# Attention and two MLPs in split fp32: query tiles and keys loaded a chunk ahead, differences in a tile of their own, weights converted in one stage

## The chip, the core and the metric

One Trainium2 chip, one of its cores. The metric is device time in microseconds (us) for one execution of the whole kernel. The core's engines run side by side, each with an instruction queue of its own that is worked off in order: TensorE (PE, matrix products), VectorE (DVE), ScalarE (ACT), GpSimd (POOL) and SyncE (SP), which in this kernel issues every DMA. An engine that stands at a semaphore holds up everything behind it in its own queue.

## What is computed

Attention of 8 heads over pooled keys and values, then two MLPs, all of it in fp32:

```python
k_p = k.reshape(B, H, S // 8, 8, D).mean(axis=3)         # B = H = 8, S = 576, D = 64
v_p = v.reshape(B, H, S // 8, 8, D).mean(axis=3)
attn = softmax(matmul(q, k_p.T) / sqrt(D))
x = matmul(attn, v_p).transpose(0, 2, 1, 3).reshape(4608, 512)
x = (sigmoid(x @ w_gate) * (x @ w_val)) @ w_out          # d_ff 1536
h = x @ w2_in                                            # d_ff 2048
out = (h * cos(h)) @ w2_out
```

The weights arrive as doubles.

## The kernel before

**Precision.** TensorE works on fp32r operands. Each fp32 number is held as a high and a low part, and a product is three matmuls: high x high, high x low, low x high. Making the two parts takes a copy on ScalarE (high) and a subtraction on VectorE (low). A weight block (128 x 512 doubles, 512 KB) takes more. ScalarE scales the exponents (`stage_exponent`, a Prelu, line 139), VectorE joins the bits (`stage_bits`, two operations, line 143), then come the high and the low part.

**Chunks and stages.** The 4608 tokens go in 9 chunks of 512. For each chunk, 12 gate steps (`gv_step`, line 515) compute 128 rows each of gate and value: 24 matmuls of 128x512 into two PSUM banks tagged "g" (four exist), a sigmoid on ScalarE, a product on VectorE. The attention of the next chunk is done beside these steps: `plan(c)` (line 580) gives for each of the 12 steps a list of calls, and the loop at line 1119 runs them behind the step's gate products. A chunk is made of the tail of one batch element and the head of the next, in 4 or 5 query tiles of up to 128 rows. For tile n at its step `at_[n]` there is `q_step` (load must be there; four transposes on TensorE, a copy qT on ScalarE), one step later `s_step` (scores; maxima and differences on VectorE, exponentials on ScalarE, the normalised a on VectorE), three steps after the first `a_step` (transposes of a; copies aT on ScalarE, low parts on VectorE). `x_step` then multiplies with the values (four products for a part of the chunk), and its results become xT. All of these use the four PSUM banks tagged "t", in turn. `q_load` is called three steps ahead of `q_step`, but not before step 0. Keys are loaded at step 0 in three groups (two of 64 pooled rows per head, one remainder of 8), pooled by GpSimd at step 1 (`kv_pool`), and transposed at step 2 (`k_step`). Values follow at steps 3 and 4.

**Differences.** For chunks 1 to 8, a gate block f and the block f + 6 are folded (`folded`, line 557). They are stored as quarters and as differences of quarters, for a product with seven instead of eight block products (`O_PRODUCTS`, line 700; the units are a third of such a product). GpSimd forms four differences, in place over the gate blocks, in two steps two ticks apart; three stores to `od` go out over three ticks. `afterwards(n, fn)` calls fn n ticks later, and a tick is a step.

**Weights converted early.** `far_weights` (line 176) is a generator. It loads a pair of blocks a and b of w2_out or w_out, converts them, forms sums of their quarters on GpSimd and converts these. One pair takes eight calls: 0 loads a; 1 loads b, Prelu of a; 2 Prelu of b; 3 bits; 4 sums, high part of a; 5 low part of a; 6 high part of b, high part of the first two sums; 7 low parts of b and of these, high part of the other two sums, whose low part opens the next call 0. The sums' results lie in the buffers of a and b, so the next pair's load waits for their store. `far_stores` issues the stores that are ready ahead of each call. Eight pairs of w2_out and six of w_out, 112 calls, run in chunks 1 to 7 at 16 a chunk (one in each step, two in each third one, lines 1143 to 1147).

**The last gate chunk and the new stage.** In chunk 8 there is no attention beside it. The blocks of w_out and w2_in are loaded there as doubles into buffers that come free, and converted beside the gate products (lines 1138 to 1151). Chunk 0's second product (`o_step`) runs there too, fed by `Ahead`, which fetches, splits and hands out blocks that were stored. Then the stage of h begins (line 1184): `h_step` for 16 blocks of each chunk, with the units of the folded product between them (`unit_go` fetches, splits and counts; `unit_step` multiplies; `due` says how many must be done by which block). The pool that held the blocks of `Ahead` is replaced by the pool of the units' operands (line 1169) when the gate stage has ended. At the end, `y_step` finishes chunk 0 of the output, and `y_chunk` does chunks 1 to 8 from seven products each. Their operands come through `strip_fetch`, `strip_high` and `strip_low`; `strip(n)` (line 917) converts up to job n and fetches one job more. `kept` (line 932) copies an accumulator out into a buffer of the ring "r", which the stored blocks y also use.

The loops that the change touches:

```python
 586      at_ = {5: (0, 2 if len(tail) == 1 else 1, 3, 5, 7), 4: (0, 2, 4, 6)}[len(tiles)]
 593          put(max(at_[n] - 3, 0), q_load, t)
1144                  for _ in range(1 + (at_f % 3 == 2)):
1145                      far_stores()
1146                      if next(far, far) is far:
1147                          load_all()
1228      strip(1)
```

Of the kernel before, what the change touches and what calls it, by code (L numbers as in the profile page):

```python
# [23 lines left out]
def attention_two_mlps(  # L24
# [22 lines left out]
    nc = tc.nc  # L47
# [39 lines left out]
    wd = [dp.tile([P, 2, DM], F32, name=f"wd{j}") for j in range(NF2)]  # L87
# [20 lines left out]
    order += [("o", f) for f in range(NF)] + [("i2", j) for j in PAIRED]  # L108
# [67 lines left out]
    def far_weights():  # L176

        def tile_(k, shape, dtype, name):
            return wp.tile(shape, dtype, tag=f"w{2 * NF + k}", name=name)

        def finished(k, kind, j, raw):
            t = tile_(k, [P, 2, DM], F32R, f"w{kind}_{j}")
            nc.scalar.copy(t[:, 0], words(raw, F32, 1))
            yield
            split_lo(nc.vector, t[:, 1], words(raw, F32, 1), t[:, 0])
            t = t.bitcast(F32)
            if kind == "o2":
                ready.append((wd[j], t))
            elif j < HF:
                ready.append((so[0][:, j], t[:, :, :HALF]))  # L190
            else:
                ready.append((so[5][:, j - HF], t[:, :, :HALF]))
                ready.append((so[6][:, j - HF], t[:, :, HALF:]))

        todo = [("o2", m, PAIRS) for m in range(PAIRS)] + [("o", m, HF) for m in range(HF)]
        for kind, m, step in todo:
            ja, jb = m, m + step
            a = load((wp, f"w{2 * NF}"), (kind, ja))
            yield
# [17 lines left out]
            for k, (op, x, y) in enumerate(sums):  # L217
                nc.gpsimd.tensor_tensor(out=t[:, k], in0=x, in1=y, op=op)
            yield from finished(3, kind, ja, a)
            yield  # L220
            both = finished(3, kind, jb, b)
            next(both)
            for k in range(2):
                c = tile_(k, [P, 2, 2, HALF], F32R, f"t{kind}{m}_{k}")
                nc.scalar.copy(c[:, :, 0], t[:, 2 * k:2 * k + 2])
                yield
                if k == 0:
                    next(both, None)
                split_lo(nc.vector, c[:, :, 1], t[:, 2 * k:2 * k + 2], c[:, :, 0])
                c = c.bitcast(F32)  # L230
                if kind == "o2":
                    ready.append((td[m][:, 2 * k:2 * k + 2], c))
                else:
                    ready.extend((so[1 + 2 * k + i][:, m], c[:, i]) for i in range(2))

    def split(upto=None, n=2):
# [13 lines left out]
        done["bits"] += len(some)  # L250

# [263 lines left out]
    def gv_step(c, f, half=None):  # L515
# [13 lines left out]
        s = gv.tile([P, C], F32, tag="s", name=f"s{c}_{f}_{cols.start}", bufs=2)[:, :n]  # L529
        nc.scalar.activation(s, pg[0], AF.Sigmoid)  # L530
# [3 lines left out]
        nc.vector.tensor_tensor(out=g[:, cols], in0=pg[1], in1=s, op=ALU.mult)  # L534
# [14 lines left out]
    def afterwards(n, fn):  # L549
        tasks.setdefault(clock[0] + n, []).append(fn)  # L550

    def tick():
        clock[0] += 1
        for fn in tasks.pop(clock[0], ()):
            fn()

    def folded(c, m, a, b):

        (a1, a2), (b1, b2) = ((x[:, :HALF], x[:, HALF:]) for x in (a, b))

        def less(out, x, y):
            nc.gpsimd.tensor_tensor(out=out, in0=x, in1=y, op=ALU.subtract)  # L562

        def put(n, t):
            nc.sync.dma_start(
                od[c][n:n + 2, :, m].rearrange("o p n -> p o n"), t.rearrange("p (o n) -> p o n", o=2)
            )

        def second():
            less(b2, b2, a1)  # L570
            less(b1, b1, b2)

        less(a1, a2, a1)
        less(a2, b2, a2)
        afterwards(1, lambda: put(5, b))
        afterwards(1, lambda: put(1, a))
        afterwards(2, second)
        afterwards(3, lambda: put(3, b))

    def plan(c):  # L580

        steps = [[] for _ in range(NF)]
        tiles = tiles_of(c)
# [36 lines left out]
        return steps  # L620
# [255 lines left out]
    def load_last():  # L876
# [4 lines left out]
        nc.sync.dma_start(t.bitcast(F32), wd[j])  # L881
# [153 lines left out]
    with tc.manual_schedule():  # L1035
# [82 lines left out]
        far = far_weights()  # L1118
        for c in range(NC):
            last = c == NC - 1  # L1120
            beside = [] if last else plan(c + 1)
            if last:
# [4 lines left out]
                load_all()  # L1127
# [3 lines left out]
            for at_f, f in enumerate(FOLDED if c else range(NF)):  # L1131
# [6 lines left out]
                elif last:  # L1138
                    if at_f >= 1:
                        go.go()  # L1140
                    split(len(raws) - 2)
                else:
                    split()
                    for _ in range(1 + (at_f % 3 == 2)):
                        far_stores()
                        if next(far, far) is far:
                            load_all()
                gv_step(c, f, 1 if c == 0 and f < FIRST else None)
                if last:
                    slots.extend(place[kind, f] for kind in "gv")  # L1150
                    load_all()
# [4 lines left out]
                if beside:  # L1156
                    for step in beside[at_f]:
                        step()
        while tasks:
            tick()  # L1160

# [3 lines left out]
        slots.extend((hp_, f"e{n}") for n in range(2))  # L1165
        load_all()
        o_homes.append((hp_, "e2"))
        last_slots.extend((hp_, f"e{n}") for n in (3, 0, 1))
        pp[0].release()
        pp[0] = tc.alloc_tile_pool(name="pp2", bufs=1, side="left", reuse_waits="tile")  # L1170
# [13 lines left out]
        for c in range(NC):  # L1184
# [8 lines left out]
            for k, j in enumerate(PAIRED):  # L1193
# [5 lines left out]
                if c == 0:  # L1199
                    split(n=1)  # L1200
                elif len(spare) < len(last_slots) and (c >= NC - 2 or k % 4 == 3):
                    load_last()
                late.append(h_step(c, j))
                if len(late) > 1:
                    late.pop(0)()
                if c < NC - 2:
# [15 lines left out]
        while tasks:  # L1222
            tick()
        load_combined(waiting.pop(0))
        while gy.next < len(gy.blocks):
            gy.go()
            y_step(*gy.take())
        strip(1)
# [37 lines left out]
```

## Time and profile before

| what | value |
|---|---|
| time, median of 3 runs (lowest to highest) | 1917.84 us (1917.09 to 1918.86) |
| the profiled execution | 1919.02 us, span 1917.2 us |
| TensorE matmuls, busy | 1789.3 us (93%), 8560 of them |
| TensorE weight loads, busy | 1491.5 us (78%) |
| VectorE, ScalarE, GpSimd, busy | 1155.9 us (60%), 928.3 us (48%), 533.2 us (28%) |
| mean granted clock of TensorE | 0.967 |
| moved by DMA | 391.20 MB, 204 GB/s |

The profile is of one execution. Busy time of TensorE is modelled and overlaps, so what counts there are the gaps and the clock. The granted clock is a share of full speed; it has two levels, 1.2 and 2.4 GHz, and a number between them is a mean over the stretch. Times of the trace are us from the start of the span. "Idle" is the time an engine stood before an instruction, with what released it behind an arrow. L66 is the line of the helper that forms all low parts.

### The profile page before, as it was taken

The page shows a single profiled execution, that of the slowest core. Times are in us where ns is not written, and L with a number is a line of the kernel's source. Part 1 is how long each engine was busy: PE and PEld are TensorE (multiplying, and loading weights), DVE is VectorE, ACT ScalarE, POOL GpSimd, SP SyncE. Part 2 cuts the span into 40 slices and gives each one's busy share as a digit, 9 for nine tenths or more (in the row PEclk, how much of TensorE's full clock was granted, in tenths as well). Part 3 has the DMA queues.
Part 4 walks back from the last instruction along what each step waited for, and adds up shares of the span by engine and source line. Part 5 has one row for each costly group of instructions (what it writes and reads, how often), then busy time and mean ns, then how long its engine had stood idle before and what let it go on. Part 6 is the DMA issues. An engine that isn't in the chain of part 4 may idle for free. (4 is left out here: it accounts for less than half of the span.)

```text
span 1917.2 us, 24961 instructions
## 1 busy us (share of the span) xinstructions
PE 1789.3 (93%) x8560; PEld 1491.5 (78%) x8560; DVE 1155.9 (60%) x1866; ACT 928.3 (48%) x1552; POOL 533.2 (28%) x656
## 2 busy tenths in 40 slices
PE   5879989898898989997999999999999998999999
PEld 4767868777777778875778888888887887888887
DVE  7675555455554645564666676676676655655665
ACT  6463434344343434343555555565564554444443
POOL 4104343535252522221001334334334441000000
PEclk8989989999999999998899999999999999999999
DMA  8424454545455544685677877777766688666664
GB/s 222 146 99 140 166 175 157 165 160 178 161 172 158 153 145 139 228 286 172 199 246 254 276 251 260 254 251 258 259 228 211 204 260 294 219 223 208 211 223 152
DMA packets 290782, 391.20 MB, mean 204 GB/s; under 512 B 55136, under 2 KB 231776, under 8 KB 290656
## 3 DMA queue, kind: packets, MB, share of 16 engines
q1 hardware_dynamic: 290656, 389.62, 62.8%
q8 instruction: 67, 1.10, 0.2%
q14 instruction: 59, 0.48, 0.1%
HBM read 242.22 MB, written 147.32 MB: 203 GB/s over the span
## 5 line engine op out<-in xcount | busy, mean ns | idle before, releaser
L534 DVE TENSOR_TENSOR g<-pv,s 128x512 f32<-128x512 f32 (+1 forms) x111 | 75.0, 676 | 282.5 <-PE pv L527 158.7
L820 DVE SCALAR_TENSOR_TENSOR r<-n,ph 128x512 f32<-128x512 int32 x144 | 98.9, 687 | 212.6 <-issue 97.8
L814 PE MATMUL ph<-x,wi 128*128 128x512 f32 x576 | 224.4, 390 | 0.0
L816 PE MATMUL ph<-x,wi 128*128 128x512 f32 x576 | 224.3, 389 | 0.0
L815 PE MATMUL ph<-x,wi 128*128 128x512 f32 x576 | 224.3, 389 | 0.0
L848 POOL TENSOR_TENSOR s<-r,r 128x256 f32<-128x256 f32 x64 | 76.1, 1189 | 467.0 <-DVE r L830 327.9
L826 ACT ACTIVATE r<-r 128x512 f32<-128x512 f32 x144 | 91.1, 633 | 236.2 <-DVE r L823 97.9
L525 PE MATMUL pg<-xT,wg 128*128 128x512 f32 (+1 forms) x444 | 188.2, 424 | 2.6 <-ACT e L443 2.6
L66 DVE TENSOR_TENSOR sp<-sf,sp 128x1024 fp32r<-128x1024 f32 x112 | 132.0, 1220 | 90.4 <-ACT sp L904 90.4
L526 PE MATMUL pg<-xT,wg 128*128 128x512 f32 (+1 forms) x444 | 179.6, 405 | 0.3 <-DVE xT L66 0.3
L527 PE MATMUL pg<-xT,wg 128*128 128x512 f32 (+1 forms) x444 | 178.6, 402 | 1.1 <-DVE wg L66 1.1
L527 PE MATMUL pv<-xT,wv 128*128 128x512 f32 (+1 forms) x444 | 170.6, 384 | 0.0
L525 PE MATMUL pv<-xT,wv 128*128 128x512 f32 (+1 forms) x444 | 170.4, 384 | 0.0
L526 PE MATMUL pv<-xT,wv 128*128 128x512 f32 (+1 forms) x444 | 170.4, 384 | 0.0
L904 ACT CAST sp<-sf 128x1024 fp32r<-128x1024 f32 x112 | 112.3, 1055 | 75.3 <-PE py_A L1007 28.6
L562 POOL TENSOR_TENSOR g<-g,g 128x256 f32<-128x256 f32 x96 | 75.7, 788 | 248.3 <-DVE g L534 139.9
L562 POOL TENSOR_TENSOR g<-g 128x256 f32<-128x256 f32 x96 | 73.4, 766 | 256.4 <-DMA od<-g 200.5
L814 PEld LDWEIGHTS ph<-x,wi 128*128 128x128 f32 x576 | 108.4, 188 | 22.6
L815 PEld LDWEIGHTS ph<-x,wi 128*128 128x128 f32 x576 | 108.3, 188 | 22.6
L816 PEld LDWEIGHTS ph<-x,wi 128*128 128x128 f32 x576 | 108.3, 188 | 22.5
L1002 PE MATMUL py_A<-tc,sp 128*128 128x512 f32 x384 | 120.6, 395 | 0.0
L530 ACT ACTIVATE s<-pg 128x512 f32<-128x512 f32 (+1 forms) x111 | 64.9, 584 | 100.3 <-PE pg L527 99.8
(180 smaller groups left out, 4227.6 us busy)
## 6 DMA issues: line engine op xcount, KB each, us to landing
sf<-sd SPq DMA_DIRECT2D x112, 512.0 KB
so<-so SPq DMA_DIRECT2D x84, 512.0 KB
uf<-od SPq DMA_DIRECT2D x168, 256.0 KB
od<-g SPq DMA_DIRECT2D x144, 256.0 KB
sd<-s SPq DMA_DIRECT2D x64, 512.0 KB
raw_o<-in_moe_w_out_dram SPq DMA_DIRECT2D x40, 512.0 KB
sd<-r SPq DMA_DIRECT2D x64, 256.0 KB
out_dram<-y SPq DMA_DIRECT2D x36, 256.0 KB
```

Of the source, the lines that this page charges most:

```text
L66: engine.tensor_tensor(out=lo, in0=x, in1=hi.bitcast(F32), op=ALU.subtract)
L525: nc.tensor.matmul(p, wh, x[:, 0, kb], start=kb == 0, stop=False)
L526: nc.tensor.matmul(p, wh, x[:, 1, kb], start=False, stop=False)
L527: nc.tensor.matmul(p, wl, x[:, 0, kb], start=False, stop=kb == KB - 1)
L562: nc.gpsimd.tensor_tensor(out=out, in0=x, in1=y, op=ALU.subtract)
L814: nc.tensor.matmul(p, wh, x[kb][:, 0], start=kb == 0, stop=False)
L815: nc.tensor.matmul(p, wh, x[kb][:, 1], start=False, stop=False)
L816: nc.tensor.matmul(p, wl, x[kb][:, 0], start=False, stop=kb == KB - 1)
L820: nc.vector.scalar_tensor_tensor(out=r, in0=n, scalar=-C1, in1=p, op0=ALU.mult, op1=ALU.add)
L826: nc.scalar.activation(r, r, AF.Sin, scale=0.5)
L904: nc.scalar.copy(t[:, 0, h * w:(h + 1) * w], got[c, n, h])
L1002: nc.tensor.matmul(p, x[:, 0, m, s], w, start=fresh and m == 0, stop=False, skip_group_check=True,)
```

## The change

- Query tiles 0 and 1 of a chunk are loaded at steps 9 and 10 of the chunk before, and key groups 0 and 1 at its step 10. Groups 0 and 1 are pooled at step 0, the remainder is still loaded at step 0 and pooled at step 1. (The plan of chunk 1 has all of these at step 0, as before.)
- GpSimd's four differences go into a tile t of their own, at the end of the next step; one store sends them two ticks later. The tile of the sigmoid is gone: it writes into g, and VectorE multiplies in place.
- `far_weights` also converts the eight pairs of w2_in (six calls a pair, no sums) and stores the finished w_out blocks whole. The calls come twice in each step of chunks 1 to 7, ahead of the gate products and behind them. `refill` then loads finished blocks in chunk 8, where nothing is converted any more.
- The pool of the units' operands is set up at the last step of chunk 8, and `unit_go` is called there twice and once behind it. `due` asks for the first units one h block later.
- `strip(1)` is called ahead of the last `y_step` instead of behind it.

```diff
+    wd = {
+        (kind, j): dp.tile([P, 2, DM], F32, name=f"w{kind}_{j}")
+        for kind, n in (("o2", NF2), ("o", NF), ("i2", NF2)) for j in range(n)
+    }
...
-    order += [("o", f) for f in range(NF)] + [("i2", j) for j in PAIRED]
...
-            if kind == "o2":
-                ready.append((wd[j], t))
-            elif j < HF:
+            ready.append((wd[kind, j], t))
+            if kind != "o":
+                return
+            if j < HF:
                 ready.append((so[0][:, j], t[:, :, :HALF]))
...
+        todo += [("i2", m, PAIRS) for m in range(PAIRS)]
...
             stage_bits([a, b])
             yield
+            if kind == "i2":
+                yield from finished(3, kind, ja, a)
+                both = finished(2, kind, jb, b)
+                next(both)
+                yield
+                next(both, None)
+                continue
...
+    refills = [("o", f) for f in range(NF)] + [("i2", j) for j in PAIRED]
+
+    def refill(tag):
+        kind, j = refills.pop(0)
+        t = wp.tile([P, 2, DM], F32R, tag=tag, name=f"w{kind}{j}")
+        nc.sync.dma_start(t.bitcast(F32), wd[kind, j])
+        blocks[kind, j] = t
+        place[kind, j] = wp, tag
...
-        s = gv.tile([P, C], F32, tag="s", name=f"s{c}_{f}_{cols.start}", bufs=2)[:, :n]
-        nc.scalar.activation(s, pg[0], AF.Sigmoid)
         g = halves.pop(f, None)
         if g is None:
             g = gv.tile([P, C], F32, tag="g", name=f"g{c}_{f}", bufs=4)
-        nc.vector.tensor_tensor(out=g[:, cols], in0=pg[1], in1=s, op=ALU.mult)
+        nc.scalar.activation(g[:, cols], pg[0], AF.Sigmoid)
+        nc.vector.tensor_tensor(out=g[:, cols], in0=pg[1], in1=g[:, cols], op=ALU.mult)
...
+    def tock():
+        for fn in tasks.pop((clock[0], True), ()):
+            fn()
...
-        less(a1, a2, a1)
-        less(a2, b2, a2)
-        afterwards(1, lambda: put(5, b))
-        afterwards(1, lambda: put(1, a))
-        afterwards(2, second)
-        afterwards(3, lambda: put(3, b))
+        def sums():
+            t = gv.tile([P, 4, HALF], F32, tag="t", name=f"tg{c}_{m}")
+            for k, x, y in ((0, a2, a1), (1, b2, a2), (3, b2, t[:, 0]), (2, b1, t[:, 3])):
+                nc.gpsimd.tensor_tensor(out=t[:, k], in0=x, in1=y, op=ALU.subtract)
+            afterwards(
+                2, lambda: nc.sync.dma_start(od[c][1:5, :, m].rearrange("o p n -> p o n"), t)
+            )
+        afterwards(1, lambda: nc.sync.dma_start(
+            od[c][5:7, :, m].rearrange("o p n -> p o n"), b.rearrange("p (o n) -> p o n", o=2)
+        ))
+        afterwards(1, sums, end=True)
...
+        def put_early(f, fn, *args):
+            early[f if c > 1 else 0].append(lambda: fn(*args))
+
         for n, t in enumerate(tiles):
-            put(max(at_[n] - 3, 0), q_load, t)
+            if n < 2:
+                put_early(NF - 3 + n, q_load, t)
+            else:
+                put(max(at_[n] - 3, 0), q_load, t)
         if c < B:
             for g in range(3):
-                put(0, kv_load, k, c, "k", g)
+                (put_early if g < 2 else put)(NF - 2 if g < 2 else 0, kv_load, k, c, "k", g)
                 put(3, kv_load, v, c, "v", g)
-                put(1, kv_pool, c, "k", g, nc.gpsimd)
+                put(1 if g == 2 or c == 1 else 0, kv_pool, c, "k", g, nc.gpsimd)
...
+        def far_step():
+            far_stores()
+            next(far, None)
+
+        plans = [plan(c) for c in range(1, NC)]
...
+            beside = [[] for _ in range(NF)]
+            if not last:
+                steps, early = plans[c]
+                for n in range(NF):
+                    if c == 0:
+                        beside[n] += early[n]
+                    beside[n] += steps[n]
+                    if c + 1 < NC - 1:
+                        beside[n] += plans[c + 1][1][n]
...
-                load_all()
+                for n in range(2 * NF, NSLOT):
+                    refill(f"w{n}")
...
                 elif last:
-                    if at_f >= 1:
-                        go.go()
-                    split(len(raws) - 2)
+                    if at_f == NF - 1:
+                        pp[0].release()
+                        pp[0] = tc.alloc_tile_pool(
+                            name="pp2", bufs=1, side="left", reuse_waits="tile"
+                        )
+                    (unit_go if at_f == NF - 1 else go.go)()
                 else:
                     split()
-                    for _ in range(1 + (at_f % 3 == 2)):
-                        far_stores()
-                        if next(far, far) is far:
-                            load_all()
+                    far_step()
                 gv_step(c, f, 1 if c == 0 and f < FIRST else None)
                 if last:
-                    slots.extend(place[kind, f] for kind in "gv")
-                    load_all()
+                    for kind in "gv":
+                        refill(place[kind, f][1])
...
+                    if at_f == NF - 1:
+                        unit_go()
+                elif c:
+                    far_step()
+                for step in beside[at_f]:
+                    step()
+                tock()
...
+            tock()
+        unit_go()
...
-                return min(TOTAL, -(-(k + 1) * TOTAL // (NF2 - 1)))
+                return max(0, min(TOTAL, -(-k * TOTAL // (NF2 - 2))))
...
-                if c == 0:
-                    split(n=1)
-                elif len(spare) < len(last_slots) and (c >= NC - 2 or k % 4 == 3):
+                if c and len(spare) < len(last_slots) and (c >= NC - 2 or k % 4 == 3):
...
             gy.go()
+            if gy.next == len(gy.blocks) - 1:
+                strip(1)
             y_step(*gy.take())
-        strip(1)
```

## Rows read from the trace of the kernel before

**Rows 1.** Waits of PE, whole span: line, released by, us in total, times, longest.
```profile
PE pq L386 <- DMA q<-in_q_dram: 31.9, 7, 5.7
PE pkr L332 <- POOL kR L286: 12.2, 6, 2.0
PE px L508 <- ACT qT L388: 8.6, 3, 6.8
```

**Rows 2.** Seven windows of the gate stage, PE: length, busy, granted clock, DMA share, GB/s.
```profile
168.00:183.00 15.00, 12.15 (x57) 0.89 0.49 129
236.00:272.00 36.00, 29.71 (x122) 0.86 0.73 214
330.00:366.00 36.00, 29.47 (x131) 0.91 0.76 223
423.00:462.00 39.00, 32.04 (x152) 0.96 0.71 214
515.00:556.00 41.00, 32.38 (x144) 0.88 0.67 198
606.00:650.00 44.00, 36.24 (x166) 0.88 0.65 188
708.00:728.00 20.00, 15.60 (x63) 0.83 0.69 216
```

**Rows 3.** Timeline of SP, steps 0 and 1 of chunk 2: start, length, issue.
```profile
237.56 0.39 SPq L174 DMA_DIRECT2D td<-to  x1
241.34 0.33 SPq L126 DMA_DIRECT2D raw_o<-in_moe_w_out_dram  x1
241.76 1.78 SPq L378 DMA_DIRECT2D q<-in_q_dram  x3
...
253.74 0.33 SPq L126 DMA_DIRECT2D raw_o<-in_moe_w_out_dram  x1
```

**Rows 4.** Timeline of PE and ACT, the same steps.
```profile
245.82 0.85 PE L386 MATMUL pq<-ident,q 128*128 128x128 f32 x4 [3.92 <-DMA q<-in_q_dram]
...
257.66 0.68 ACT L141 ACTIVATE raw_o<-raw_o 128x512 f32<-128x512 f32 x1 [0.75 <-DMA raw_o<-in_moe_w_out_dram]
```

**Rows 5.** Chunks 1 to 7, busy PE, PEld, DVE, ACT, POOL; two groups by form.
```profile
158.00:797.00 639.00, 589.30 (x2805) 487.06 (x2804) 346.99 (x686) 272.00 (x467) 257.84 (x330) 0.95 0.50 158
...
L141 ACT ACTIVATE raw_i<-raw_i 128x512 f32<-128x512 f32 x16 | 10.0, 665 | 0.0
...
L66 DVE TENSOR_TENSOR wi<-raw_i,wi 128x512 fp32r<-128x512 f32 x16 | 12.2, 785 | 0.0
```

**Rows 6.** Timeline of POOL, the key remainder of chunk 3, in step 1.
```profile
261.09 1.76 POOL L286 TENSOR_TENSOR raw_k<-raw_k 64x256 f32<-64x256 f32 x2
262.93 0.65 POOL L286 TENSOR_TENSOR kR<-raw_k 64x64 f32<-64x64 f32 x1
```

**Rows 7.** Waits of SP's queue and of ACT, whole span: total, times, longest.
```profile
SPq L126 <- DMA td<-to: 60.5, 16, 5.3
...
ACT raw_o L141 <- DMA raw_o<-in_moe_w_out_dram: 37.0, 18, 5.8
```

**Rows 8.** The stage of h begins: timeline of PE and SP, and a window of PE.
```profile
909.53 0.80 PE L770 MATMUL po_A<-up,so 128*128 128x512 f32 x1 [13.69 <-ACT up L730]
...
902.12 2.12 SPq L739 DMA_DIRECT2D uf<-od  x4
...
905.00:942.00 37.00, 28.72 (x100) 0.77 0.62 205
```

**Rows 9.** The stage of y begins: timeline of PE and ACT; DMA, 1570 to 1620.
```profile
1604.35 1.22 PE L1002 MATMUL py_B<-tc,sp 128*128 128x512 f32 x2 [5.95 <-ACT sp L904]
...
1611.93 0.63 PE L1002 MATMUL py_A<-tc,sp 128*128 128x512 f32 x2
...
1607.83 1.17 ACT L935 COPY m<-py_A 128x512 f32<-128x512 f32 x2 [2.59 <-DMA out_dram<-y]
...
DMA packets 7346, 16.03 MB, mean 321 GB/s; under 512 B 590, under 2 KB 4046, under 8 KB 7343
```

More of the change, by code (lines that the diff above doesn't have):

```diff
@@ L86, in attention_two_mlps @@
     sd = {c: dp.tile([7, P, PAIRS, HALF], F32, name=f"sd{c}") for c in range(1, NC)}
-    wd = [dp.tile([P, 2, DM], F32, name=f"wd{j}") for j in range(NF2)]
+    wd = {
+        (kind, j): dp.tile([P, 2, DM], F32, name=f"w{kind}_{j}")
+        for kind, n in (("o2", NF2), ("o", NF), ("i2", NF2)) for j in range(n)
+    }
     td = [dp.tile([P, 4, 2, HALF], F32, name=f"td{m}") for m in range(PAIRS)]
@@ L547, in attention_two_mlps, with afterwards @@
     clock = [0]
-    def afterwards(n, fn):
-        tasks.setdefault(clock[0] + n, []).append(fn)
+    def afterwards(n, fn, end=False):
+        tasks.setdefault((clock[0] + n, end), []).append(fn)
     def tick():
         clock[0] += 1
-        for fn in tasks.pop(clock[0], ()):
+        for fn in tasks.pop((clock[0], False), ()):
+            fn()
+    def tock():
+        for fn in tasks.pop((clock[0], True), ()):
             fn()
@@ L559, in folded @@
         (a1, a2), (b1, b2) = ((x[:, :HALF], x[:, HALF:]) for x in (a, b))
[L561 to L566, printed above, removed]
-            )
-        def second():
-            less(b2, b2, a1)
-            less(b1, b1, b2)
-        less(a1, a2, a1)
-        less(a2, b2, a2)
-        afterwards(1, lambda: put(5, b))
-        afterwards(1, lambda: put(1, a))
-        afterwards(2, second)
-        afterwards(3, lambda: put(3, b))
+        def sums():
[4 more added lines that the diff above has]
+                2, lambda: nc.sync.dma_start(od[c][1:5, :, m].rearrange("o p n -> p o n"), t)
+            )
+        afterwards(1, lambda: nc.sync.dma_start(
+            od[c][5:7, :, m].rearrange("o p n -> p o n"), b.rearrange("p (o n) -> p o n", o=2)
+        ))
+        afterwards(1, sums, end=True)
     def plan(c):
         steps = [[] for _ in range(NF)]
+        early = [[] for _ in range(NF)]
         tiles = tiles_of(c)
@@ L619, in plan @@
             put(f, fn, *args)
-        return steps
+        return steps, early
     x2 = {}
@@ L1118, in attention_two_mlps @@
         far = far_weights()
+        def far_step():
+            far_stores()
+            next(far, None)
+        plans = [plan(c) for c in range(1, NC)]
         for c in range(NC):
             last = c == NC - 1
-            beside = [] if last else plan(c + 1)
-            if last:
+            beside = [[] for _ in range(NF)]
[7 more added lines that the diff above has]
+                        beside[n] += plans[c + 1][1][n]
+            else:
                 far_stores()
@@ L1155, in attention_two_mlps @@
                         o_next()
-                if beside:
-                    for step in beside[at_f]:
-                        step()
+                    if at_f == NF - 1:
[5 more added lines that the diff above has]
+                tock()
         while tasks:
             tick()
+            tock()
+        unit_go()
         gv.release()
         hp_ = tc.alloc_tile_pool(name="hp", bufs=1, side="right", reuse_waits="tile")
-        slots.extend((hp_, f"e{n}") for n in range(2))
-        load_all()
         o_homes.append((hp_, "e2"))
         last_slots.extend((hp_, f"e{n}") for n in (3, 0, 1))
-        pp[0].release()
-        pp[0] = tc.alloc_tile_pool(name="pp2", bufs=1, side="left", reuse_waits="tile")
         TOTAL = len(O_PRODUCTS) * STEPS
@@ L1223, in attention_two_mlps @@
             tick()
+            tock()
         load_combined(waiting.pop(0))
```

3 lines of the change are left out of this document (2 added, 1 removed).

## The prediction

> **What bounds the kernel now.** I read first the waits of TensorE, then the windows around the stalls, then the queues that feed them. TensorE is the bound: everything that is computed goes through it, and no product is added or taken away. So the change is worth what it takes off TensorE's idle time and off the stretches that follow at the lower clock. [rows 1] shows two waits that come back once a chunk: the transposes of a query tile wait for its load (31.9 us in 7 times; the first, in the opening, is not touched here), and the transpose of the key remainder waits for GpSimd's pooling (six times, up to 2.0 us). [rows 2] has the seven stretches of the gate stage around these waits. In each row the length less PE's busy time is idle time, and the length times what the granted clock lacks to 1.0 is what the lower of the two levels (1.2 instead of 2.4 GHz) costs. Idle: 2.85 + 6.29 + 6.53 + 6.96 + 8.62 + 7.76 + 4.40 = 43.4 us. Clock: 1.65 + 5.04 + 3.24 + 1.56 + 4.92 + 5.28 + 3.40 = 25.1 us. Together **68.5 us**. [rows 3] and [rows 4] show why the query is late: the load leaves SyncE's queue at 241.76, inside the step that needs it, behind a weight load that itself waited for a store.
>
> **The sum is made against the profiled execution**, 1919.0 us with a span of 1917.2; it stands 1.2 us above the median of the three runs, 1917.84.
>
> **Part 1: query tiles 0 and 1 and key groups 0 and 1 loaded a chunk ahead.** q moves from step 0 to steps 9 and 10 of the chunk before, two or three steps early, where a step takes 639 / 84 = 7.6 us [rows 5]. The four transfers and more pass the stores of the same queue, but a late q now has some 15 us of slack. The query wait ends. Keys 0 and 1 land two steps early and are pooled in step 0, so GpSimd has only the remainder left in step 1: 1.76 + 0.65 = 2.4 us [rows 6]. The remainder's load stays in step 0, though, and in chunks 2 to 5 both weight calls of that step now stand ahead of it on SyncE. Before, the first blocked SyncE until 241.34 and the second came a step later (until 253.74, [rows 3]). After, the second store wait, 3.8 us in the mean and 5.3 at most [rows 7], comes at once: the load leaves near 248, lands about 4 us later and is pooled near 254.5. TensorE reached that transpose 2.0 us before 263.58, at 261.5, and will reach it some 6 us earlier without the query stall: 255.5. Margin 1 us. Taken: **-68.5, and +3** for remainders that are late; bounds 0 and 4 x (2.0 + 1.6) = 14.
>
> **Part 2: differences in their own tile.** The same four GpSimd operations, one store of four quarters instead of two of two; GpSimd no longer waits for a store before it overwrites, and SyncE's store waits for nothing late (two ticks behind). The sigmoid now writes into g's buffer, so ScalarE waits for a buffer of four; its last reader, the differences, ran two steps earlier. Nothing on the path: 0, covered by GpSimd's idle time, 639 - 258 us [rows 5].
>
> **Part 3: all weights converted in the gate stage.** Sixteen w2_in blocks move there: two ScalarE operations of 0.67 us and three VectorE operations of at most 0.79 each [rows 5], 21 us and at most 38 us, in a stretch where these engines idle 367 and 292 us. As work they are hidden. The twelve w_out blocks are no longer converted twice. What matters is the **spacing of the calls**. A pair of w_out or w2_out blocks takes eight calls; these came 16 to a chunk and now come two in every step, one ahead of the gate products and one behind. Call 0 loads block a, after a wait for the store of the tile that held its buffer; call 1 loads b and puts a's Prelu on ScalarE. Before, a whole step lay between a load and its Prelu; now half of one does. Store 3.4 us (237.56 + 0.39 to 241.34), load 3.9 us (253.74 to 257.66) [rows 3, 4]: the chain of 7.3 us starts only when the last step's g is done, and the Prelu reaches ScalarE 3.8 us later. So ScalarE stands some 3.5 us in call 1, and about as long in call 2 for block b (store and load again, against half a step). The longest such wait so far is 5.8 us, all of them 37.0 [rows 7]. Behind ScalarE's wait queue the sigmoid (four banks, two steps of cover), the copy qT, the exponentials and the copies aT.
>
> TensorE meets it where a step has five users of the four "t" banks: one query tile and four x products, the fifth of which needs qT's copy done. That is so in chunk 1 (step 4) and chunk 2 (step 5), and in chunks 3 and 4 the x products wait for aT a step behind. The kind of wait exists already: px behind qT, 8.6 us in three times [rows 1]. Taken: 4 chunks x (2.6 us idle + 1.4 us clock) = **+16**. Bounds: 0, as the slack may hold; 45, if each of the 13 pairs after the first passes the 3.5 us on. From chunk 5, step 8, the calls are for w2_in, whose loads wait for no store: 0.
>
> The Trainium skill, page "SBUF — State Buffer", section "The DMA setup-cost knee", gives a transfer about 2 us plus its bytes at 436 GB/s; my estimate from it is 3.2 us for 512 KB, 6.4 us for the chain. By that page the lag would be 1 us smaller and this term +12. The measured 3.4 and 3.9 us decide.
>
> **Part 4: the new product's operands sooner.** TensorE stands from 895.8 to 909.5, 13.7 us [rows 8]: the first fetch leaves SyncE at 902.12, behind stores and raw loads. Now it leaves a step earlier, ahead of chunk 8's last gate products, and the first units come after two blocks of h, not one. In the window 905 to 942 there are 8.3 us idle, 4.5 of them the same wait, so 3.8 more; clock 0.23 x 37 = 8.5 us, of which 2.3 fall in the idle part. Total 13.7 + 3.8 + 6.2 = 23.7. The second unit's fetch still leaves behind the last weight load, which waits for TensorE, and is 1 to 4 us late. Taken **-21**; bounds -24 and -10.
>
> **Part 5: strip(1) ahead of the last y_step.** The wait of product B, 5.95 us, ends. But the next product (py_A at 1611.93) needs accumulator A copied out, and that copy started only at 1607.83, behind the store of y whose buffer it takes [rows 9]. Its own operand is converted behind that copy on ScalarE. The move puts strip(1)'s fetch, 1 MB, ahead of those stores on SyncE, in a stretch where the DMA engines moved 321 GB/s [rows 9]: about 3 us later. So the copy starts near 1610.7, the product near 1614, not at 1611.93; the wait goes from B to A and grows. Taken **+2**; bounds -8 (B's wait and its clock gone, nothing behind it) and +6 (twice the fetch).
>
> **Sum:** -68.5 + 3 + 16 - 21 + 2 = -68.5; 1919.0 - 68.5 = 1850.5, and 1.2 lower on the scale of the median: **1849 us**.
>
> **Rivals.**
> Clean: ScalarE's waits stay covered, term 3 is 0, the remainder is never late, the stage start gives 23.7. -68.5 - 23.7 + 2 = -90: **1828**. For it: in 37.0 us of such waits so far TensorE stood for little. Against: half the distance. Chance 0.25.
> Not what it says: hoisted loads still leave late, as SyncE is in order and stands in every fourth step for two stores. Then the query wait stays, 26.9 us and some 13 of the clock: 1849 + 40 = **1889**. Against: two steps of slack. Chance 0.06.
> Slower: ScalarE's waits for converted weights become TensorE's in every pair. It decides when a pair costs TensorE over 84.5 / 14 = 6.0 us (84.5 being the gain without the 16 of part 3). At both longest waits [rows 7], 5.8 + 5.3, less 3 of slack, it is 8.1 x 14 = 113, and 1918 - 84.5 + 113 = **1946**. For it: PSUM has two steps of cover and no more. Against: ScalarE is idle 57% of the stage. Chance 0.05.
>
> **How the numbers follow.** The forecast has 0.60, clean 0.25, the two others 0.11, 0.04 lies elsewhere. All bounds at their best give 1919 - 68.5 - 24 - 8 - 1 = 1817, at their worst -68.5 + 14 + 45 - 10 + 6 = -13.5, 1904. The range 1815 to 1888 holds the forecast, the clean case and the lower half of the bad end. A measurement of this kernel tells apart about 0.2%, 4 us. Faster: forecast, clean, not-what-it-says and most of the rest, 0.93; same 0.02; slower 0.05.
>
> **What would show it.** Right: no wait of pq for q beyond the first 5 us, key remainder waits near nothing; px waits of 2 to 4 us behind qT or aT in chunks 1 to 4; longer waits of ScalarE's Prelu for raw_o; po_A's first wait under 4 us; no wait of py_B, but one of 8 to 11 us ahead of py_A's second product. Wrong: the pq waits still there; gate stretches without any px wait (then 1828); a wait at each fourth step; py_A's second product at once.

## The result and the profile after

The changed kernel takes **1942.72 us** (median of 4 runs, 1939.25 to 1949.19) against 1918.21 for the kernel before (4 runs, 1917.09 to 1918.86): a ratio of **1.0132, interval 1.0105 to 1.0159**. It is slower, by 24.5 us or 1.3%, and the interval lies wholly above 1. 1849 was forecast.

| profiled execution | before | after |
|---|---|---|
| time; span | 1919.02; 1917.2 us | 1939.25; 1937.4 us |
| VectorE, ScalarE, GpSimd, busy | 1155.9, 928.3, 533.2 us | 1128.1, 908.8, 548.7 us |
| mean granted clock | 0.967 | 0.962 |
| moved by DMA | 391.20 MB, 204 GB/s | 414.28 MB, 214 GB/s |

The work of VectorE and ScalarE became less, as the change says, and the time did not. The stages tell where. These are the windows of TensorE after, cut at the first gate product of a chunk, the first product of h and the first of y (start:end, length, busy, granted clock, DMA share, GB/s): chunks 1 to 5, chunks 6 and 7, chunk 8, the stage of h, the stage of y.

```profile
151.60:654.30 502.70, 431.92 (x2022) 0.92 0.60 191
654.30:821.30 167.00, 164.34 (x792) 0.98 0.57 181
821.30:919.18 97.88, 97.88 (x433) 1.00 0.76 249
919.18:1609.07 689.89, 672.77 (x2930) 0.99 0.75 246
1609.07:1937.40 328.33, 315.54 (x1793) 0.98 0.64 211
```

Cut in the same way, the kernel before has these; the first line counts 421.04 us busy at a clock of 0.96:

```profile
152.20:608.60 456.40, 421.04 (x2024) 0.96 0.52 162
608.60:793.00 184.40, 170.06 (x793) 0.94 0.48 151
793.00:892.96 99.96, 98.29 (x434) 1.00 0.77 255
892.96:1592.68 699.72, 674.22 (x2930) 0.98 0.74 245
1592.68:1917.20 324.52, 314.39 (x1793) 0.99 0.64 213
```

Four differences are gains or small: -17.4 in chunks 6 and 7, -2.1 in chunk 8, -9.8 in the stage of h, +3.8 at the end. One decides: **chunks 1 to 5 grew by 46.3 us**. There TensorE stands 35.4 us longer (502.70 - 431.92 against 456.40 - 421.04), and the same products (2022 and 2024 records of them) count 10.9 us more of busy time, at a granted clock of 0.92 instead of 0.96.

The waits of TensorE after (line, released by, us in total, times, longest) show which wait went and which came:

```profile
PE pg L545 <- ACT xT L529: 30.8, 5, 7.8
PE psc L419 <- ACT qT L408: 16.9, 4, 7.3
...
PE px L528 <- ACT qT L408: 12.8, 3, 6.8
...
PE pq L406 <- DMA q<-in_q_dram: 3.4, 1, 3.4
```

The query's wait of [rows 1], 31.9 us, is down to the 3.4 us of the opening, and the key remainder's 12.2 us are gone. In their place stand the first gate product of a chunk, which waits for ScalarE's copy xT, and the scores, which wait for ScalarE's copy qT: 47.7 us together. The waits of ScalarE say why these copies are late:

```profile
ACT raw_o L143 <- DMA raw_o<-in_moe_w_out_dram: 108.1, 24, 9.3
...
ACT raw_i L143 <- DMA raw_i<-in_moe_w_in_dram: 42.2, 13, 6.0
...
ACT wo L185 <- DMA so<-wo: 29.8, 6, 8.1
ACT wo L185 <- DMA wo<-wo: 29.4, 6, 8.5
```

The Prelu (L143) waits 108.1 us for doubles of w2_out and w_out that are not there yet (37.0 in [rows 7]) and 42.2 for those of w2_in. The high-part copies (L185) wait for stores that must leave their target first, 29.8 and 29.4 us. Before, these two were:

```profile
ACT wo L183 <- DMA wd<-wo: 29.2, 8, 6.3
...
ACT wo L183 <- DMA so<-wo: 13.7, 4, 6.0
```

The first of the five stalls, at the end of chunk 1, can be followed instruction by instruction. ScalarE, VectorE, SyncE and TensorE (start, length, line, operation; in brackets how long it stood before it and for what):

```profile
233.22 0.65 ACT L143 ACTIVATE raw_o<-raw_o 128x512 f32<-128x512 f32 x1 [7.75 <-DMA raw_o<-in_moe_w_out_dram]
...
246.04 0.66 ACT L185 CAST wo<-raw_o 128x512 fp32r<-128x512 f32 x1 [8.50 <-DMA wo<-wo]
...
249.19 0.62 ACT L236 CAST to<-to 128x512 fp32r<-128x512 f32 x1 [1.49 <-DVE wo L66]
249.72 1.61 ACT L529 CAST xT<-px 128x384 fp32r<-128x384 f32 x4
...
238.64 1.22 DVE L66 TENSOR_TENSOR wo<-raw_o,wo 128x512 fp32r<-128x512 f32 x1
...
236.20 4.05 SPq L319 DMA_DIRECT2D raw_k<-in_k_dram  x4
...
241.00 0.36 SPq L176 DMA_DIRECT2D wo<-wo  x1
...
250.24 0.79 PE L545 MATMUL pg<-xT,wg 128*128 128x512 f32 x1 [7.27 <-ACT xT L529]
```

Read from below. TensorE stands 7.27 us for xT. xT is an eviction (a copy out of PSUM) of 1.6 us, but it stands in ScalarE's queue behind the weight calls 6 and 7. The copy of call 6 waited 8.50 us for the store of block a, which had to leave the buffer that block b's copy writes. That store left SyncE at 241.00, behind the issues of the hoisted key loads (4.05 us). The low part that it carries was ready at 239.86, so the place in SyncE's queue cost it 1.1 us at most. From the end of its issue it took 4.7 us. Of the 7.27 us, 3.1 pass while ScalarE still stands at that copy, and 3.7 with what comes between it and xT: the two copies of sums, a sigmoid and a further wait of 1.49 us.

### The profile page after: what moved, and what is told of

The parts are those of the page before. It is cut to its first block, busy times and chain, and to the rows that moved or that the text cites. A ratio compares the mean times of both kernels' runs of the same rounds, so it can differ in the third digit from the quotient of the medians.

```text
span 1937.4 us, 24756 instructions
## 1 busy us (share of the span) xinstructions
PE 1794.7 (93%) x8560; PEld 1496.4 (77%) x8560; DVE 1128.1 (58%) x1830; ACT 908.8 (47%) x1528; POOL 548.7 (28%) x656
## 2 busy tenths in 40 slices
DMA packets 296350, 414.28 MB, mean 214 GB/s; under 512 B 55072, under 2 KB 231712, under 8 KB 296224
## 5 line engine op out<-in xcount | busy, mean ns | idle before, releaser
L553 DVE TENSOR_TENSOR g<-pv,g 128x512 f32<-128x512 f32 (+1 forms) x111 | 75.1, 676 | 336.8 <-ACT g L552 141.4
L545 PE MATMUL pg<-xT,wg 128*128 128x512 f32 (+1 forms) x444 | 188.4, 424 | 35.2 <-ACT xT L529 30.8
L872 POOL TENSOR_TENSOR s<-r,r 128x256 f32<-128x256 f32 x64 | 76.1, 1188 | 453.6 <-DVE r L854 328.3
L545 PEld LDWEIGHTS pg<-xT,wg 128*128 128x128 f32 x444 | 89.3, 201 | 54.2 <-ACT xT L529 31.9
L840 PEld LDWEIGHTS ph<-x,wi 128*128 128x128 f32 x576 | 108.1, 188 | 22.5
L839 PEld LDWEIGHTS ph<-x,wi 128*128 128x128 f32 x576 | 108.1, 188 | 22.4
L552 ACT ACTIVATE g<-pg 128x512 f32<-128x512 f32 (+1 forms) x111 | 64.9, 585 | 116.6 <-PE pg L547 61.2
L847 DVE SCALAR_TENSOR_TENSOR r<-n,r 128x512 f32<-128x512 int32 x144 | 107.8, 749 | 5.0
```

Source lines behind the costliest of these rows:

```text
L545: nc.tensor.matmul(p, wh, x[:, 0, kb], start=kb == 0, stop=False)
L839: nc.tensor.matmul(p, wh, x[kb][:, 1], start=False, stop=False)
L840: nc.tensor.matmul(p, wl, x[kb][:, 0], start=False, stop=kb == KB - 1)
L847: nc.vector.scalar_tensor_tensor(out=r, in0=n, scalar=-C2, in1=r, op0=ALU.mult, op1=ALU.add)
```

## The experiments

Each ratio is to executions of the kernel before on the same chip; experiment 6 was executed once and has none. The stages are cut as above, each from one profiled execution.

**1. The change without part 3.** The calls come 16 a chunk again, and w_out and w2_in are converted beside the last gate chunk and the first h blocks again. The first theory: the new pace of the weight calls and their new places cost the time. The rival: the hoisted loads do, by standing ahead of the weight stores on SyncE and in the DMA engines.

```diff
-        todo += [("i2", m, PAIRS) for m in range(PAIRS)]
...
-                    far_step()
+                    for _ in range(1 + (at_f % 3 == 2)):
+                        far_stores()
+                        if next(far, far) is far:
+                            load_all()
...
-                elif c:
-                    far_step()
```

> The kernel after with part 3 undone: w_out and w2_in are converted beside the last gate chunk and the first h blocks again, and the calls of the weight generator come 16 a chunk, ahead of the gate products. Theory 1 (the pace of the calls: ScalarE stands for stores and loads of weight blocks, and TensorE behind it): the stretch of chunks 1 to 5, 503 us after and 456 us before, falls to about 400 to 415, and the time to 1835 to 1855 us. Theory 2 (the loads that were moved ahead stand on SyncE and in the DMA engines in front of the weights' stores): the waits of ScalarE for stores stay long, and the time stays above 1900 us.

Measured 1859.03 us, ratio 0.9702 (0.9676 to 0.9727). That is above the 1835 to 1855 expected; the window of chunks 1 to 5 is as expected. That window, and waits of TensorE and ScalarE:

```profile
151.70:566.00 414.30, 407.39 (x2023) 0.99 0.56 179
...
PE pg L544 <- ACT xT L528: 4.7, 3, 1.9
...
ACT raw_o L144 <- DMA raw_o<-in_moe_w_out_dram: 30.7, 20, 5.4
```

So part 3 costs 84.6 us of span (1937.4 - 1852.8): 88.4 in chunks 1 to 5, and 3.8 come back elsewhere. The 88.4 are 63.9 more idle time (70.8 against 6.9) and 24.5 more busy time at the lower clock. The rest of the change is worth some -60 us: -58 by the medians, -64.4 by the two profiled spans.

**2. The change without the hoist**, the rival's own test.

```diff
-            if n < 2:
-                put_early(NF - 3 + n, q_load, t)
-            else:
-                put(max(at_[n] - 3, 0), q_load, t)
+            put(max(at_[n] - 3, 0), q_load, t)
...
-                (put_early if g < 2 else put)(NF - 2 if g < 2 else 0, kv_load, k, c, "k", g)
+                put(0, kv_load, k, c, "k", g)
```

> The kernel after with part 1 undone: all q and k loads in their own chunk again, pooling at step 1. Theory 1: the waits for weight blocks stay, the waits for q and for the key remainder come back on top: 1955 to 1985 us. Theory 2: the wait of the xT copies at the chunk's end (31 us in five times) goes, the q waits (27 us) come back: 1930 to 1945 us.

Measured 1965.76 us, ratio 1.0257 (1.0234 to 1.028): 23 us slower than the change, not faster. TensorE waits for the query again, and for xT still. Below these two waits stand the store of block a and the copy behind it at the end of chunk 1:

```profile
PE pq L406 <- DMA q<-in_q_dram: 32.3, 5, 8.6
PE pg L545 <- ACT xT L529: 20.6, 5, 4.9
...
242.34 0.33 SPq L176 DMA_DIRECT2D wo<-wo  x1
...
245.05 0.65 ACT L185 CAST wo<-raw_o 128x512 fp32r<-128x512 f32 x1 [5.07 <-DMA wo<-wo]
```

The rival falls as the main cause. It has a share: without the hoist the xT waits come to 20.6 us instead of 30.8, and this store takes 2.4 us from the end of its issue instead of 4.7. At the ends of chunks 2 to 4 the copy gets its buffer 2.4 to 2.7 us from the end of the last store's issue here, and 4.7 to 5.3 us after. So the hoisted loads lengthen the transfer of these stores; their place in SyncE's queue cost the first 1.1 us at most.

**3. The pace alone**: experiment 1 with its 112 calls once ahead of the gate products and once behind, and no w2_in and no whole w_out blocks.

```diff
-                    for _ in range(1 + (at_f % 3 == 2)):
-                        far_stores()
-                        if next(far, far) is far:
-                            load_all()
+                    far_stores()
+                    next(far, None)
...
+                elif c:
+                    far_stores()
+                    next(far, None)
```

> e1_weights_as_before, but its 112 weight calls (w2_out and w_out only, no w2_in, no whole w_out blocks) come twice in each step, one ahead of the gate products and one ahead of the attention, as in the kernel after; they are through in chunk 5. If the pace is the cause: chunks 1 to 5, 414 us in e1 and 503 after, come out at 480 to 505, and the time at 1925 to 1950 us. If what was added (sixteen blocks of w2_in, the whole stores of w_out) is the cause: chunks 1 to 5 under 430, 1855 to 1880 us.

Measured 1926.55 us, ratio 1.0036 (1.0022 to 1.005), chunks 1 to 5 at 488.70, as the theory of the pace expected:

```profile
151.40:640.10 488.70, 432.84 (x2023) 0.92 0.57 178
...
PE pg L544 <- ACT xT L528: 24.8, 4, 7.2
...
ACT raw_o L144 <- DMA raw_o<-in_moe_w_out_dram: 101.5, 25, 7.8
```

Of the 88.4 us, 74.4 (488.7 - 414.3) come with the pace alone; the other 14 come with the blocks of w2_in and the whole w_out stores. The work that was added is the smaller part of the cost. The pace is two things that this run doesn't part: the calls stand half a step apart, and all 112 of them fall into chunks 1 to 5, where experiment 1 has 80.

**4. Both calls of a step behind the attention work**, at the change's pace. The work stays; what differs is what stands behind the calls on ScalarE, and the distance between the two calls of a step.

```diff
-                    far_step()
...
-                elif c:
-                    far_step()
...
+                if c and not last:
+                    far_step()
+                    far_step()
```

> The kernel after with both weight calls of a step put behind the step's attention work (they were one ahead of the gate products, one ahead of the attention). Nothing else. Theory 1: the copies qT, aT and xT no longer stand behind a Prelu or a copy that waits for a DMA in the same step; the waits of TensorE for xT (30.8 us) and qT (29.7 us) shrink to under a third, 1880 to 1910 us. Theory 2: stores and loads are as late as before, and so is ScalarE: within 10 us of 1943.

Measured 1881.11 us, ratio 0.9807 (0.9787 to 0.9828), 62 us faster than the change. Chunks 1 to 5, ScalarE's waits for weight blocks, and TensorE's for qT:

```profile
152.90:600.00 447.10, 420.68 (x2023) 0.96 0.65 209
...
ACT raw_o L143 <- DMA raw_o<-in_moe_w_out_dram: 91.2, 24, 8.6
...
ACT raw_i L143 <- DMA raw_i<-in_moe_w_in_dram: 35.7, 11, 6.0
...
ACT wo L185 <- DMA so<-wo: 24.5, 5, 6.8
...
ACT wo L185 <- DMA wo<-wo: 15.9, 5, 5.8
...
PE psc L419 <- ACT qT L408: 4.7, 4, 1.5
```

This is the run to look at. By these four rows ScalarE stands a fifth less than after (167.3 against 209.5 us), while TensorE's idle time in chunks 1 to 5 falls by more than half, from 70.8 to 26.4. Its wait for xT is gone (the trace has no such row), and that for qT ahead of the scores falls from 16.9 to 4.7; the x products still wait 12.0 us for qT (12.8 after), so the waits for qT come to 16.7 of 29.7 us, not under the third that was expected. So the cost lies less in how long ScalarE stands than in **what stands behind it in its queue**. One reserve: two calls in one place are also spaced otherwise than two half a step apart, and ScalarE does stand less, so this run doesn't part the place wholly from the waits.

**5. The Prelu of a half a step later**, at the change's places.

```diff
+            yield
             stage_exponent(a)
-            yield
             stage_exponent(b)
```

> The kernel after with the Prelu of block a moved from call 1 to call 2, so a whole step lies behind its load instead of half of one; block b's stays half a step behind its load. If the pace is the cause: ScalarE's waits of the Prelu for raw_o, 108 us, fall to 60 to 85 and the time by 10 to 40 us, to 1903 to 1933. If it is the amount of work and traffic: within 6 us of 1943.

Measured 1931.2 us, ratio 1.0059 (1.0039 to 1.0078): 11.5 us less than the change. The Prelu's waits fall to 85.9 us, just above the 60 to 85 expected, and TensorE's for xT from 30.8 to 24.1. But the transposes of the query (pq) now stand 17.8 us where the profile names no releaser, 1.3 after. The lag between block a's load and its Prelu is a cause, but a small one; block b's lag and the stores' waits stay.

**6. strip(1) back behind the last y_step**, executed once.

```diff
-            if gy.next == len(gy.blocks) - 1:
-                strip(1)
...
+        strip(1)
```

> The kernel after with strip(1) behind the last y_step again. From the first product A to the second, which took 19.25 us before and 20.07 after: my part 5 expects 19.3 again; if the move had brought anything, it would be 21 or more.

Measured 1941.81 us. From the first product A to the second it takes 19.71 us, between the 19.25 of before and the 20.07 after. From the first product A to the end it takes 325.0 us instead of 328.3; before it was 324.5. The wait is back at product B (6.0 us) and gone from the second product A. The move of part 5 costs 3.3 us. After, the chain looks like this (TensorE, ScalarE, SyncE):

```profile
1622.31 0.73 PE L1026 MATMUL py_B<-tc,sp 128*128 128x512 f32 x2 [2.64 <-DMA tc<-td]
1629.14 1.22 PE L1026 MATMUL py_A<-tc,sp 128*128 128x512 f32 x2 [5.87 <-ACT sp L928]
...
1626.92 1.23 ACT L959 COPY m<-py_A 128x512 f32<-128x512 f32 x2 [7.34 <-DMA out_dram<-y]
...
1617.30 0.88 SPq L919 DMA_DIRECT2D sf<-sd  x2
1618.28 2.48 SPq L1057 DMA_DIRECT2D out_dram<-y  x4
```

The copy of A waits 7.34 us for the store of y, which now leaves behind strip(1)'s fetch; the operand sp is converted behind that copy.

**7. The kernel before with part 1 alone.**

> The kernel before with part 1 alone (query tiles 0 and 1 and key groups 0 and 1 a chunk ahead, these pooled at step 0). My part 1, by its 68.5 us less late remainders: 1850 to 1862 us. A rival: with the differences still in place, GpSimd stands for a store before it can pool at step 0, and the key waits stay: 1875 us or more.

Measured 1871.4 us, ratio 0.9757 (0.9742 to 0.9772). The hoist by itself is worth 48 us, not 65: both expectations missed, with the time between them. Its waits of TensorE show part of what it gives back, small waits for xT of the same kind, 8.3 us, already at the old pace (the start of the h stage stays as late as it was, with a wait of 13.9 us):

```profile
PE pg L525 <- ACT xT L509: 8.3, 4, 2.8
```

Chunks 1 to 7 take 589.2 us here and 578.4 in experiment 1, which also has part 2 (and parts 4 and 5, which act later). So the new tile for the differences is worth about 11 us. That is one profile of each; the first kernel of experiment 8, which has part 2 too, takes 576.2.

**8. The parts that gain, then the calls moved.** First experiment 1 with strip(1) back and `due` as before; then that kernel with its weight calls, at the old 16 a chunk, behind the attention work.

```diff
-                    for _ in range(1 + (at_f % 3 == 2)):
-                        far_stores()
-                        if next(far, far) is far:
-                            load_all()
...
+                if c and not last:
+                    for _ in range(1 + (at_f % 3 == 2)):
+                        far_stores()
+                        if next(far, far) is far:
+                            load_all()
```

> e1_weights_as_before with strip(1) back behind the last y_step and with due as before: 3.3 us from the strip, and po waits for up of 0.9 instead of 2.1 us, some 4 us: 1850 to 1855 us. A rival: the later first units are what shortened the first wait of po_A, and that grows again by what is won.

> e8_best with its weight calls (16 a chunk, the pace of the kernel before) put behind the step's attention work. If the place of the calls counts at any pace, the four or five small waits that are left in chunks 1 to 6 (xT, qT, aT: some 11 us with the clock) shrink: 1840 to 1847 us. A rival: at this pace the copies are rarely late, and a call behind the attention delays the next step's sigmoid instead: within 4 us of 1850.

The first: 1849.96 us, ratio 0.9645 (0.9629 to 0.9662). The second: **1838.58 us, ratio 0.9585 (0.956 to 0.9611)**, the fastest of all. Between the two only the place of the calls differs, and chunks 1 to 5 go from 413.4 to 403.7 us, where TensorE hardly stands any more (2.0 us) and the granted clock is 1.00. ScalarE's waits in the first; then, of the second, the window of chunks 1 to 5 and what is left of these waits:

```profile
ACT raw_o L144 <- DMA raw_o<-in_moe_w_out_dram: 32.4, 21, 5.0
ACT wo L186 <- DMA wo<-wo: 31.7, 6, 8.3
...
151.40:555.10 403.70, 401.67 (x2016) 1.00 0.58 183
...
ACT raw_o L144 <- DMA raw_o<-in_moe_w_out_dram: 11.5, 6, 6.9
...
ACT wo L186 <- DMA wo<-wo: 4.7, 2, 2.8
```

At the old pace, then, the move also takes away most of ScalarE's standing. Why it stands less there wasn't tried, so this pair of runs shows what the place is worth, and not that it acts through the order in the queue alone.

**9. The whole change, repaired**: experiment 4 with strip(1) back and `due` as before.

> e3_calls_last (all weights converted in the gate stage, calls behind the attention work) with strip(1) back and due as before: 3.3 us from the strip, 3 from due, 1872 to 1878 us. If it came near 1850, the conversion in the gate stage would cost nothing once its calls stand last; I expect that 20 us and more stay, as ScalarE still waits some 90 us for raw_o.

Measured 1873.79 us, ratio 0.977 (0.974 to 0.9799). It has the shortest h stage (688.0 us; nothing is converted there), but chunks 1 to 5 take 445.1 where the fastest kernel takes 403.7. ScalarE still waits 89.7 us there for doubles of w2_out and w_out, against 11.5: at 24 calls a chunk TensorE still pays for conversion in the gate stage, even behind the attention work.

## Why the prediction was wrong

The forecast was wrong in sign. What came is nearest to its own third rival, "ScalarE's waits for converted weights become TensorE's in every pair", with 1946 against 1942.7 measured, to which it gave 0.05. That the two numbers are so near is luck. The rival has part 3 at 113 us, measured 84.6, and the other parts at -84.5, measured some -60; and TensorE stood not in every pair but mostly at nine places, five for xT and four for qT.

**The step that failed is the size of part 3's term.** Forecast +16, bounds 0 and 45; measured +84.6 (experiment 1), with 74.4 of the 88.4 in chunks 1 to 5 from the pace (experiment 3). The mechanism was named: half a step between load and Prelu, ScalarE standing, copies queued behind it. What failed is the cover that TensorE was given, and with it the places where it would stand.

- *Where TensorE meets it.* The prediction counted steps with five users of the "t" banks and priced "4 chunks x (2.6 us idle + 1.4 us clock)". It followed qT, aT and the sigmoid, and gave the sigmoid "two steps of cover". At the x products, where it looked, the wait for qT grew from 8.6 us to 12.8. But at the end of a chunk the copy xT stands in the same queue, and the very next gate product needs it. That place alone gave 30.8 us of idle time in 5 times, the scores behind qT 16.9 more.
- *Which wait stands there.* Its 3.5 us for the Prelu in calls 1 and 2 were near the mean: 108.1 us in 24 times are 4.5 each, but 9.3 the longest. It did not price call 6, whose high-part copy of b writes into the buffer that a's store, issued in the same call, must first leave. Four of the five stalls for xT stand behind that copy; it waited 8.50, 6.79, 8.07 and 7.34 us. The fifth stands behind a Prelu of w2_in.
- *How late ScalarE comes to it.* The length of that wait is not its price. In experiment 1 the same copy waits almost as long at the end of chunk 1, and the gate product behind it hardly stands:

```profile
229.73 0.65 ACT L186 CAST wo<-raw_o 128x512 fp32r<-128x512 f32 x1 [8.33 <-DMA wo<-wo]
...
232.80 0.50 PE L544 MATMUL pg<-xT,wg 128*128 128x512 f32 x1 [1.12 <-ACT xT L528]
```

There ScalarE came to the copy at 221.40, 10.3 us before TensorE needed xT; after, it came at 237.54, 5.4 us before, soon behind a Prelu that had stood 7.75 us. As far as this place shows, it is waits one behind the other, where TensorE has little slack, that the term left out.

The estimate from the Trainium skill's page "SBUF — State Buffer", section "The DMA setup-cost knee", 3.2 us for 512 KB, fits neither store shown: from the end of its issue the one at the end of chunk 1 took 4.7 us after, at a DMA share of 0.52 in that chunk, and 2.4 us without the hoist (experiment 2). The 3.4 us that the prediction took from the rows of before were too short for the first of them as well; that part 1's loads would lengthen a store stood in no term.

**Part 1** (-68.5 + 3): right in kind, too large. The query wait and the remainder's wait went exactly as said, and the late remainder did not come. Alone it measured -48 (experiment 7). Two things made it too large. Its clock term, 25.1 us, takes the whole length of each window, idle part and all; by the way of part 4, which takes the idle part out, it would be 4.8 us less. And the whole idle time of the seven windows was taken as removable. Once TensorE is not late for the query, ScalarE's copies are late for it (8.3 us for xT). What makes up the rest stays open.

**Part 2** (0): it measured about -11 us, one profile each. The step "Nothing on the path" was wrong if that holds. Which of its three edits brings it (GpSimd's waits, the stores, the sigmoid's buffer) wasn't tried and stays open.

**Part 3, w2_in** ("0"): chunk 7 is as short after as in experiment 1 (77.7 us both), so work for w2_in there is hidden, as said. But its Prelu waits 42.2 us in all, and at the end of chunk 5 one such wait of 6.0 us stands ahead of xT, for which TensorE stands 3.1. Up to chunk 5 w2_in and the whole w_out stores together cost 14 us.

**Part 4** (-21, bounds -24 and -10): mis-sized. From the first h product to the first y product experiment 1 takes 570.4 us, 4.0 less than the 574.4 of before, and the change 564.2, 10.2 less; the 6.2 between them come with part 3, which leaves no conversion to the first h chunk. (The clock inside the idle part was put at 2.3 us there; 0.23 of 8.3 us is 1.9.) The wait of 13.69 us [rows 8] did go: the first units start without one. But a later unit waits 3.39 us, and SyncE shows why (TensorE, then SyncE):

```profile
936.34 0.79 PE L794 MATMUL po_A<-up,so 128*128 128x512 f32 x1 [3.39 <-ACT up L754]
...
930.36 0.36 SPq L589 DMA_DIRECT2D od<-tg  x1
930.81 2.58 SPq L763 DMA_DIRECT2D uf<-od  x4
```

Its fetch leaves right behind a store of differences (L589), for which SyncE had stood 8.5 us until GpSimd was done with tile tg. The prediction had named another late unit, "behind the last weight load"; this store, which part 2 makes one of four quarters and which waits for all four differences, it had not followed into this stage. And `due`, one block later, leaves the units less lead: with it back, the same stretch is 2.8 us shorter (567.6 in the first kernel of experiment 8 against 570.4).

**Part 5** (+2): right in place and nearly in size. The wait went from B to A, 5.95 to 5.87 us, and the move costs 3.3 us. The forecast "8 to 11 us" for A's wait was too long, since B now waits 2.64 us for another operand first.

The parts by their measured sizes: -48 (part 1), -11 (part 2), -4 (part 4, in experiment 1), +4 (part 5, experiment 1's end against before), +84.6 (part 3 with its gain in the h stage) give +26 against +20.2 us of span. The 6 us left are what the parts do to one another; chunk 8 is one such place, 97.9 us after and in experiment 1, 100.3 with part 1 alone.

## What to carry to other kernels

Before you call work on an idle engine hidden, write down that engine's queue in order and find, for each instruction that may wait for a transfer, the next evictions behind it and how much slack their consumer has; the least slack counts, not the mean. Put instructions that wait for DMA behind those that the critical engine needs: the same work moved a few lines down was worth 62 us at the change's pace and 11 at the old one, whether by the order alone or also by shorter waits. And when several edits come together, price them singly: here a gain of some 60 us was buried by one term that none of the others needed.

## What was not expected

- Idle time cost more than itself. In chunks 1 to 5, 63.9 us more of idle time (after against experiment 1) came with 24.5 us more of busy time for the same products, with the granted clock at 0.92 instead of 0.99: 0.38 us for each us that TensorE stood, as a mean of this stretch. Where it hardly stood (the fastest kernel, 2.0 us in 403.7) the clock is 1.00.
- ScalarE's standing is a poor measure of the cost: 167.3 us of waits for weight blocks (experiment 4) go with chunks 1 to 5 that are 55.6 us shorter than with 209.5 us (after). The waits of an engine beside the path can't be added up as a price; when they come, and what stands behind them in its queue, has a large part in it.
- Loads that were moved off the path still count as traffic: beside the hoisted loads a 512 KB store took 4.7 us from the end of its issue, without them 2.4.
